# Moving the last three waits of a DMA-bound kernel from SP to GpSimd

## The chip, the cores and the metric

The kernel runs on one core of one Trainium2 chip. The metric is the device time of one execution in microseconds, as it is reported for each run. All runs quoted were fast, with a granted clock of 1.0. The *span* that the profile shows is a different quantity: it runs from the first to the last instruction of the program.

## The reference

```python
B, S, D = 1024, 16, 512          # bfloat16
def reference(x, y, gamma):      # x, y: (B, S, D); gamma: (D,)
    return x + gamma * y
```

Two arrays of 16.8 MB are read and one is written, with one multiplication and one addition for each element.

## The kernel before

The program is written by hand, with one instruction stream for each engine. SP issues the loads, ACT issues the load of gamma and the two stores, VectorE (DVE) multiplies and adds, TensorE (PE) only broadcasts gamma and passes two signals on. GpSimd (POOL) has, apart from its part in the opening barriers and one instruction called INC_SWDGE_SEM, nothing but four small fills that the framework puts at the opening of the program. A helper waits for a semaphore and takes its count off again:

```python
def _take(sem, n, eng):
    return eng.wait_ge(sem, n).then_inc(sem, -n)        # line 25 of the profile
...
SP = [('y', 0, 64), ('x', 0, 64, 0), ('y', 64, 128), ('x', 64, 117, 0), ('x', 117, 128, 64)]
ACT = [('g',), ('s', 0, 64), ('s', 64, 128)]
...
    ring(nc.sync, SP, EARLY[0])      # issues the loads; the first goes ahead of the opening barriers
    ring(nc.scalar, ACT, EARLY[1])   # issues gamma and, when its rows are added, each store
    nc.vector.memset(ones_row, 1.0).then_inc(s_ones, 1)
...
    nc.scalar.sem_inc(s_end, 1)                      # ACT has issued everything
    _take(s_end, 1, nc.sync)
    _take(s_add, n, nc.sync)                         # all additions are done
    _take(s_out, 16 * len(stores), nc.sync)          # both stores have landed: the end of the program
```

The last line holds back the end of the program until all 32 increments of the two stores are in: the last of them came 118.571 us after the span's start, and SP's wait ended at 118.604.

Of the kernel before, what the change touches and what calls it, by code (L numbers as in the profile page):

```python
# [21 lines left out]
def _take(sem, n, eng):  # L22


    return eng.wait_ge(sem, n).then_inc(sem, -n)  # L25


def kernel(
# [9 lines left out]
    nc = tc.nc  # L38
# [9 lines left out]
    n = len(PIECES)  # L48
# [13 lines left out]
    stores = [w for w in SP + ACT if w[0] == "s"]  # L62
# [9 lines left out]
    s_add, s_go, s_rel, s_end, s_out = sem("s_add"), sem("s_go"), sem("s_rel"), sem("s_end"), sem("s_out")  # L72
# [93 lines left out]


    nc.scalar.sem_inc(s_end, 1)
    _take(s_end, 1, nc.sync)
    _take(s_add, n, nc.sync)  # L170
    _take(s_out, 16 * len(stores), nc.sync)

    main = nc.main_func.blocks[0].instructions
    names = {i.name for i in early}
# [35 lines left out]
```

## Time and profile before

| | kernel before |
|---|---|
| reported time, median of 3 | 119.94 us (119.87 to 119.99) |
| span | 118.6 us |
| last of 32 store increments, from the span's start | 118.571 us |
| DMA traffic | 50.33 MB at 424 GB/s over the span; DMA share 0.99, 1.01 and 1.01 in the three stretches of 30 us up to 90 us |
| VectorE busy | 59% |

The lines that the prediction rests on stand in it. The page's groups of DMA issues (what it writes and reads, queue, count, and at the end the median time from issue to landing in us) have this line for the two stores, the second of which is the last transfer:

```profile
out_dram<-y_sb ACTq DMA_DIRECT2D x2, 22.8
```

The opening, in the timeline (start, duration, engine, line, operation):

```profile
0.00 0.37 SPq L116 DMA_DIRECT2D y_sb<-in_y_dram  x1
0.23 0.10 POOL L194 MEMSET const-float32-0.0<- 128x1 f32 x1 [0.23 <-issue]
...
1.52 0.17 DVE L127 MEMSET ones_row<- 1x128 bf16 x1 [1.52 <-PEq L41]
```

The span starts with SP's first load issue. The first instruction that touches data on an engine is GpSimd's fill at 0.23 us, the next VectorE's fill at 1.52.

### The profile page before, as it was taken

What the parts mean: (1) busy time and instruction counts of PE and PEld (TensorE: products, weight loads), DVE (VectorE), ACT (ScalarE), POOL (GpSimd) and SP (SyncE); (2) the same over time, 40 slices, a digit from 0 to 9 for tenths busy, and PEclk for the clock granted to TensorE, in tenths of its full rate; (3) what the DMA queues carried; (4) which work ended last, traced back from release to release, by engine and by line L of the source; (5) the groups of instructions that cost most, each with busy time, mean ns of one, the idle gap of its engine ahead of it and who ended that gap; (6) DMA issues with size and microseconds to landing.
All of it is one profiled execution on the core that took longest, in us unless ns stands there. A gap on an engine that the chain in (4) does not pass through costs nothing. (4 is left out here: it accounts for less than half of the span.)

```text
span 118.6 us, 78 instructions
## 1 busy us (share of the span) xinstructions
PE 0.6 (0%) x1; PEld 0.1 (0%) x1; DVE 70.0 (59%) x10; POOL 0.2 (0%) x4
## 2 busy tenths in 40 slices
PE   0001000000000000000000000000000000000000
PEld 0000000000000000000000000000000000000000
DVE  0002000599999299999759999999999910000000
POOL 0000000000000000000000000000000000000000
DMA  9889888998899888998896969598899888988892
GB/s 354 354 376 685 354 354 354 597 464 354 354 398 663 354 354 354 663 398 354 354 586 293 586 293 567 220 639 354 354 575 486 354 354 376 685 354 354 354 619 88
DMA packets 1010, 50.33 MB, mean 424 GB/s; under 512 B 113, under 2 KB 114, under 8 KB 114
## 3 DMA queue, kind: packets, MB, share of 16 engines
q1 hardware_dynamic: 720, 33.55, 66.0%
q10 hardware_dynamic: 290, 16.78, 32.6%
HBM read 33.56 MB, written 16.78 MB: 424 GB/s over the span
## 5 line engine op out<-in xcount | busy, mean ns | idle before, releaser
L156 DVE TENSOR_TENSOR y_sb<-y_sb,gamma_sb 128x27136 bf16<-128x27136 bf16 (+1 forms) x4 | 34.6, 8688 | 12.7 <-DVEq L25 12.7
L165 DVE TENSOR_TENSOR y_sb<-x_sb,y_sb 128x27136 bf16<-128x27136 bf16 (+1 forms) x4 | 34.6, 8688 | 2.3 <-DVEq L25 2.2
L132 DVE CAST gamma_sb<-gamma_ps 128x512 bf16<-128x512 f32 x1 | 0.7, 692 | 8.8 <-DVEq L25 8.8
L127 DVE MEMSET ones_row<- 1x128 bf16 x1 | 0.2, 165 | 1.5 <-PEq L41 1.5
L130 PE MATMUL gamma_ps<-gamma_row,ones_row 1*128 1x512 bf16 x1 | 0.6, 578 | 9.7 <-PEq L25 9.7
L130 PEld LDWEIGHTS gamma_ps<-gamma_row,ones_row 1*128 1x128 bf16 x1 | 0.1, 100 | 9.7 <-issue 9.7
L194 POOL MEMSET const-uint8-127<- 128x1 uint8 x1 | 0.1, 102 | 0.0
L194 POOL MEMSET const-bfloat16-1.0<- 128x1 bf16 x1 | 0.1, 101 | 0.0
L194 POOL MEMSET const-float32-0.0<- 128x1 f32 x1 | 0.1, 98 | 0.2 <-issue 0.2
L194 POOL MEMSET const-float32-1.0<- 128x1 f32 x1 | 0.1, 98 | 0.0
## 6 DMA issues: line engine op xcount, KB each, us to landing
x_sb<-in_x_dram SPq DMA_DIRECT2D x1, 6784.0 KB, 20.8
x_sb<-in_x_dram SPq DMA_DIRECT2D x1, 1408.0 KB, 23.9
y_sb<-in_y_dram SPq DMA_DIRECT2D x2, 40.2
out_dram<-y_sb ACTq DMA_DIRECT2D x2, 22.8
x_sb<-in_x_dram SPq DMA_DIRECT2D x1, 39.7
gamma_row<-in_gamma_dram ACTq DMA_DIRECT2D x1, 1.0 KB
```

The lines of the kernel that those rows point to most:

```text
L127: nc.vector.memset(ones_row, 1.0).then_inc(s_ones, 1)
L130: nc.tensor.matmul(gamma_ps, ones_row, gamma_row, start=True, stop=True).then_inc(s_ps, 1)
L132: nc.vector.tensor_copy(out=gamma_sb, in_=gamma_ps).then_inc(s_dve, 1)
L156: nc.vector.tensor_tensor(out=yt, in0=yt, in1=g, op=MULT).then_inc(s_dve, 1)
L165: nc.vector.tensor_tensor(out=yt, in0=xt, in1=yt, op=ADD).then_inc(s_add, 1)
L194: nc = _bacc.Bacc("TRN2", target_bir_lowering=False, num_devices=1)
```

## The change

GpSimd is idle for the whole body (0.2 us busy, in the four fills, the last of which ends at 0.43 us), so it is to do the waiting. SP then ends with its last load, issued at 56.1 us.

```diff
     nc.scalar.sem_inc(s_end, 1)
-    _take(s_end, 1, nc.sync)
-    _take(s_add, n, nc.sync)
-    _take(s_out, 16 * len(stores), nc.sync)
+    _take(s_end, 1, nc.gpsimd)
+    _take(s_add, n, nc.gpsimd)
+    _take(s_out, 16 * len(stores), nc.gpsimd)
```

## The prediction

The marks, here and in two of the expectations, show where passages are cut. The records show clearing in blocks of consecutive numbers, of which that of 7 to 53 ends last (119.117 to 119.465 us), but not which engine clears which.

> **What bounds the kernel now.** I read the page from the top, then the same end of the span cut into stretches, then SP's own waits, then the line that holds every wait, and last the semaphore records that lie behind these views. First the header and the slices:
>
> ```profile
> span 118.6 us, 78 instructions
> ...
> DVE  0002000599999299999759999999999910000000
> POOL 0000000000000000000000000000000000000000
> DMA  9889888998899888998896969598899888988892
> GB/s 354 354 376 685 354 354 354 597 464 354 354 398 663 354 354 354 663 398 354 354 586 293 586 293 567 220 639 354 354 575 486 354 354 376 685 354 354 354 619 88
> DMA packets 1010, 50.33 MB, mean 424 GB/s; under 512 B 113, under 2 KB 114, under 8 KB 114
> ```
>
> The DMA row is full from the first slice to the last but one, while VectorE is idle in the last seven slices and GpSimd all along. So 50.33 MB of traffic sets the time, and what comes after it is a tail. The stretches at the end (columns: length, busy time of PE, PEld, DVE and POOL, clock, DMA share, GB/s):
>
> ```profile
> 95.00:98.00 3.00, 0.00 (x0) 0.00 (x0) 0.36 (x1) 0.00 (x0) 1.00 0.81 350
> 98.00:118.00 20.00, 0.00 (x0) 0.00 (x0) 0.00 (x0) 0.00 (x0) 1.00 0.97 419
> 117.00:118.60 1.60, 0.00 (x0) 0.00 (x0) 0.00 (x0) 0.00 (x0) 1.00 0.01 0
> ```
>
> From 98 us on nothing runs but the second store. It was issued by ACT at 95.40 us and takes some 23 us. Who waits for it is in the DMA queue's own waits and in the line of the waits:
>
> ```profile
> SPq L25 <- SPq L25: 62.0, 2, 39.3
> ...
> L25 DVEq EVENT_SEMAPHORE  x9: 21/21/21, 10.4 to 80.0; - x9
> L25 PEldq EVENT_SEMAPHORE  x3: 51/51/51, 1.7 to 76.6; - x3
> L25 SPq EVENT_SEMAPHORE  x3: 17/17/17, 95.8 to 118.6; - x3
> L25 ACTq EVENT_SEMAPHORE  x1: 17/17/17, 76.8 to 76.8; - x1
> ```
>
> SP's three waits are those at issue: the first two pass at 95.8 us, right behind ACT's last issue, and the third, for the stores, at 118.6 us, which is where the span ends. (The releaser named in the wait view is a program line, not the store; the landing records below show the store.) The chain of waits adds nothing here: its last entry is the last addition.
>
> The rest I take from the trace's semaphore records, in us from the span's start. The last of the 32 store increments lands at 118.571; SP's wait runs from 118.587 to 118.604. The span stops there, but the reported time, 119.93 for the profiled execution, is 1.33 longer. What follows in the records: five updates of semaphore 2 at 118.736, 118.779, 118.817, 118.852 and 118.899; then all other semaphores cleared, from 118.849 to 119.465; then nine more updates of semaphore 2, from 119.689 to 120.046. So the tail behind the last store is about 1.4 us, and the reported time evidently contains most of it. The change can act only on this tail.
>
> [...]the nine updates at the end span 357 ns, and the clearing falls into five interleaved blocks of about 51 numbers.[...]GpSimd's waits in the opening barriers took 17 ns[...].[...] the records show 2 x 16 increments, so either engine has to wait for the same last one.
>
> **The change part by part.** The order of shown instructions is the same on all engines; only three waits move from SP to GpSimd.
>
> 1. First two waits: they pass at about 95.8 us, 22.8 us before the last landing. Cost 0 on either engine.
>
> 2. SP ends early. Its last load is issued at 56.1 us, and then it has only the closing barrier to wait in. ACT shows that this is safe: it issues the last store at 95.40 and, by the records, steps into the barrier at 96.01, while the store runs on for 22.6 us. I expect 0 for the transfers.
>
> 3. The third wait on GpSimd. In the opening barriers, before the body, an engine's wait starts some time after the increment that releases it: 25 ns on GpSimd (update at one record, wait at the next), 17 on SP. Start to start of two waits in a row is 78 ns on GpSimd and 70 on SP. From landing to SP's step into the barrier it is 118.736 - 118.571 = 165 ns. GpSimd's analogue: 165 + 8 + 8 = 181. Added: 0.016 us.
>
> 4. The order of the barrier, where I expect the cost. The first update of semaphore 2 in the body comes 0.235 us after PE's last instruction, the second 0.224 after ACT's, the next two follow 39 and 43 ns later, and the fifth, alone, comes after SP's wait. So the order up is PE, ACT, GpSimd, DVE, SP, and down again DVE, GpSimd, ACT, PE (which engine is third and which fourth[...] is an inference). SP is the turning point. When it comes last, only the way down is left: 118.736 to 118.899, 163 ns. With GpSimd last, its own step up, DVE's step up, SP's turn and the whole way down are left. The records have such a case, in the barrier 2.7 us before the span's start, where the third update came late: its seven remaining updates follow at 43, 24, 112, 39, 34 and 50 ns, in sum 302 ns. The long 112 is DVE's: it had just stepped up and needs 136 ns from there to its next step, though SP's turn is in the middle. Added: 302 - 163 = 0.139 us.
>
> 5. PE is the last to leave the first barrier,[...] and is the first that the final barrier needs (119.689). So a later release of PE moves everything behind it one for one.
>
> Sum: 0.016 + 0.139 = 0.155 us on 119.94, that is **120.10 us**, 0.13% longer.
>
> **The rivals.** (a) *Nothing arrives.* If the reported time ends with the last wait, or the waiting hides the step up, only the 0.016 us of term 3 remain: 119.95. For it: the origin of the 1.33 us is my reading. Against: a figure that stops at the wait would be near 118.6. (b) *SP has work of its own after its program*, which it now does early, hidden. The 132 ns from the end of its wait to its barrier step is the most it could be; a gain of at most 0.1, 119.84. Against: PE and ACT show even longer gaps (235 and 224 ns), so this is probably common to all engines and GpSimd would have it too. (c) *GpSimd ends heavily*: one of its drains in the opening took 181 ns against 8 on ACT. If such a thing stands on its way out, it adds another 0.15 to 0.2: 120.3. Its later drains, with no memsets before them, took 41 and 34 ns, which speaks against. (d) *The transfers shift* because SP has gone: a new order on the queues could move the last landing by a few tenths either way, 119.6 to 120.3. Step 2 speaks against, and the issue order does not change.
>
> **Range and chances.** The three timings of before lie from 119.87 to 119.99, so 0.06 either way is plain scatter, less for a median. Term 4 is measured on one event and rests on an inferred order; it could be 0 or, with (c), double. I take 119.90 to 120.35. A change of over 2% would be 2.4 us, longer than the whole 1.4 us tail, so a gain of that size is impossible from the tail, and a loss would need something that no record shows. Faster 0.004, same 0.986, slower 0.010.
>
> **What would show it right or wrong.** Right: the last store increment at the same 118.57 within a tenth or two; GpSimd's third wait within 30 ns of it; semaphore 2 then stepping up three times more and down four times, with a gap over 100 ns in the middle, some 0.30 us in all instead of 0.163; the clearing and final barrier unchanged in shape and later by that much; and the span itself, which ends at the wait, almost unchanged (118.6). Term 3 is wrong if GpSimd takes over 60 ns longer than SP from landing to barrier. Term 4 is wrong if four updates follow GpSimd's as they followed SP's. Step 2 is wrong if the landings of loads or stores moved by more than the scatter. The prediction fails if the time is below 119.90, which would point to (b) or (d), or above 120.35, which would point to (c).

## The result, and the profile after

The changed kernel took 120.66 us (median of 6 runs, 120.57 to 120.77) against 119.97 us (119.87 to 120.01) of the kernel before in the same rounds. The ratio is 1.0058, with a 95% interval from 1.0045 to 1.0071. A ratio here is the mean time of one kernel's fast runs over that of the other's of the same rounds, so it isn't quite the ratio of the medians. The change is within 2%, but clearly slower, by 0.69 us where 0.16 was predicted, and outside the predicted range.

The page of the changed kernel, first the header and the slices:

```profile
span 118.8 us, 78 instructions
...
DVE  0002000699999299999759999999999910000000
POOL 0000000000000000000000000000000000000000
DMA  9899888998899888988896979598899888988891
GB/s 353 353 420 640 353 353 353 662 397 353 353 530 530 353 353 375 684 353 353 353 585 292 548 329 548 238 638 353 353 552 508 353 353 375 684 353 353 353 662 44
```

Slice by slice it's nearly the kernel before. The span grew by 0.2 us only, not by 0.69. The stretches at the end (length, busy time of PE, PEld, DVE and POOL, clock, DMA share, GB/s) are as before too:

```profile
95.00:98.00 3.00, 0.00 (x0) 0.00 (x0) 0.41 (x1) 0.00 (x0) 1.00 0.81 350
98.00:118.00 20.00, 0.00 (x0) 0.00 (x0) 0.00 (x0) 0.00 (x0) 1.00 0.97 419
117.00:118.80 1.80, 0.00 (x0) 0.00 (x0) 0.00 (x0) 0.00 (x0) 1.00 0.01 0
```

The line of the waits shows that the change was made as meant, and that the last wait still ends the span (engine, count, duration in ns, first and last start):

```profile
L25 DVEq EVENT_SEMAPHORE  x9: 21/21/21, 10.2 to 80.1; - x9
L25 PEldq EVENT_SEMAPHORE  x3: 51/51/51, 1.7 to 76.8; - x3
L25 POOLq EVENT_SEMAPHORE  x3: 17/17/17, 95.9 to 118.8; - x3
L25 ACTq EVENT_SEMAPHORE  x1: 17/17/17, 77.0 to 77.0; - x1
```

SP's row is gone, and POOL has it, with the same 17 ns. None of these views shows where 0.5 us went. It lies behind the span, in the semaphore records of the trace. After its last instruction each engine steps into a barrier, seen as updates of semaphore 2. There are nine of them for five engines: the first five are the engines' steps up, and the other four, within 163 ns of SP's step in before, are read as the same order down again. In the changed kernel two come before GpSimd's (77.388 and 96.050 us) and six follow it. With the last landing as the origin, the tail divides as follows, in ns:

| part of the tail | before (SP waits) | after (GpSimd waits) | difference |
|---|---|---|---|
| last landing to the start of the wait | 16 | 23 | +7 |
| the wait instruction | 17 | 17 | 0 |
| end of the wait to the waiter's step into the barrier (its *exit*) | 132 | 562 | +430 |
| from that step to the last step of the barrier | 163 | 285 | +122 |
| clearing of semaphores, up to the final barrier's first step | 790 | 788 | -2 |
| the final barrier | 357 | 357 | 0 |
| sum | 1475 | 2032 | +557 |

So 0.557 of the 0.69 us are in the tail, and 0.43 of them between GpSimd's last instruction and its next sign of life. The other 0.13 us would be in the body: the last store landed 118.756 us after the span's start, 0.185 later than before in these two single profiles.

### The profile page after: what moved, and what is told of

Its sections match the earlier page's. It is cut to its first block, busy times and chain, and to the rows that moved or that the text cites. A ratio compares the mean times of both kernels' runs of the same rounds, so it can differ in the third digit from the quotient of the medians.

```text
span 118.8 us, 78 instructions
## 1 busy us (share of the span) xinstructions
PE 0.6 (0%) x1; PEld 0.1 (0%) x1; DVE 70.0 (59%) x10; POOL 0.2 (0%) x4
```

## The experiments

The theory after the result (A, later G1): GpSimd has a fixed exit of 0.56 us, where SP has 0.13, and the rest of the tail is the barrier's order. Its rivals: all engines but SP are like that (B); GpSimd is slow to go on after a long wait (G2); its exit is long because it ran the opening fills (G3); its exit is work that it could also do while it waits or between simple instructions (G4); it is a cost of being last (G5); it undoes what its opening instruction set up (G6). For the 0.13 us in the body there was scatter (S) against an effect of SP's early end (T). Eleven runs were made, on two chips, all with correct results; each is compared with the kernel before.

### c_before: the kernel before, unchanged

> The kernel before once more, unchanged, for the spans of its executions. In the profile of the change the span (to the end of the last wait) was 118.80 us against 118.60, and the last store landed 118.756 us after the span's start against 118.571. Theory S (scatter[...]): the spans of this run lie between 118.5 and 118.9 and overlap with those of the change (118.7 to 118.9), so that the 0.19 us need no cause. Rival T (the change slows the transfers): all spans here lie at 118.5 to 118.65. Time 119.9 to 120.0, and time less span 1.33 us under both.

It took 120.14 us (119.93 to 120.26, 6 runs), against 120.11 us (119.99 to 120.5, 11 runs) of the same kernel; ratio 0.9997. The six spans lie from 118.6 to 118.9 us, and those of the eleven runs beside it from 118.7 to 119.2. Time less span was 1.28 to 1.37 us throughout, while the spans wandered. So executions of one and the same kernel differ by more than the 0.13 us in question; theory S holds so far. The expected time, 119.9 to 120.0 us, was missed, and the eleven runs beside it go over the band of expected spans at the top. The scatter of 0.06 us that the prediction had taken from three runs was too small too.

### end_act, end_dve, end_pe: the same three waits on the other engines

```diff
-    _take(s_end, 1, nc.sync)              # and the two waits behind it
+    _take(s_end, 1, nc.scalar)            # end_act; nc.vector: end_dve; nc.tensor: end_pe
```

> ACT takes the three last waits. Theory A (GpSimd alone has some 0.43 us of exit between its wait and its step into the barrier; the other engines have SP's 0.13 to at most 0.24): ACT steps 0.13 to 0.24 us after the end of its wait, the barrier then needs 0.32 us instead of SP's 0.163 (the way up from ACT and all the way down), time 120.1 to 120.25. Rival B (SP is the exception, every engine with a datapath pays some 0.56): the step comes 0.5 us or more after the wait, time 120.5 to 120.7.

> VectorE takes the three last waits. Theory A: the step comes 0.13 to 0.24 us after the end of the wait, the barrier then needs 0.24 us (SP's turn and the way down, with DVE's own pause of some 0.1), time 120.0 to 120.2. Rival B: step after 0.5 us or more, time 120.4 to 120.6.

> TensorE takes the three last waits. Theory A: the step comes 0.13 to 0.24 us after the end of the wait, the barrier then needs all its 0.36 us, time 120.15 to 120.35. Rival B: step after 0.5 us or more, time 120.55 to 120.75.

All three ran beside c_before. By the semaphore records, in ns:

| waiter | exit | step to end of the barrier | tail | time, us (median) | ratio to before (95%) |
|---|---|---|---|---|---|
| SP (c_before) | 132 | 163 | 1476 | 120.14 | 0.9997 (0.9984 to 1.0010) |
| DVE (end_dve) | 183 | 241 | 1617 | 120.27 | 1.0008 (0.9994 to 1.0023) |
| ACT (end_act) | 145 | 322 | 1650 | 120.16 | 1.0000 (0.9983 to 1.0017) |
| PE (end_pe) | 235 | 357 | 1816 | 120.34 | 1.0015 (1.0000 to 1.0029) |
| GpSimd (the change) | 562 | 285 | 2032 | 120.66 | 1.0058 (1.0045 to 1.0071) |

The last row is from the first comparison. It was run at another time. Each exit is from one profiled run; those of SP and GpSimd came out the same to 1 ns in every other run where that engine waits last.

Rival B falls: three more engines have exits of 145 to 235 ns, and only GpSimd needs 562. The barrier's part behaves as the order PE, ACT, GpSimd, DVE, SP says: the earlier an engine's place, the more steps are left when it comes last (357, 322, 285, 241 and 163 ns). The order itself, of which two places were an inference, is now shown: in end_dve two steps stand right behind ACT's end (96.18 and 96.22 us) and only the fourth waits for VectorE, and in end_pe none comes before PE's. The times alone would not have decided it; ACT's 0.17 us longer tail doesn't show in its ratio, because the spans happened to be short. The records of the tail repeat to a few ns (1473 to 1476 in the four profiles in which SP waits last), the times to a few tenths of a us (119.99 to 120.5 in the eleven runs beside these).

### c_after: the change once more

> The kernel of the change once more, unchanged. The tail from the last landing to the last update of semaphore 2 should again be 2.03 us against 1.475 of before (0.56 more), and time less span 1.87 against 1.33. Theory S (the transfers are not touched, their 0.19 us in the first profiles was scatter): over the timed executions the spans of this kernel and of before have means within 0.1 us of each other and the ratio of times is 1.0046, 0.56 us. Rival T (SP's early end slows the transfers too): spans longer by 0.1 to 0.2 us, ratio 1.0055 or more.

It took 120.59 us (120.50 to 120.78, 5 runs) against 120.01 us (119.91 to 120.5, 9 runs); ratio 1.0049 (1.0036 to 1.0063). The tail was 2032 ns again, with an exit of 562. The mean span was 118.72 us in its 5 runs and 118.76 in the 9 of the kernel before, and time less span was 1.84 to 1.91 against 1.29 to 1.36. The difference is thus in the tail, 0.56 us, and none of it shows in the transfers. Five spans against nine, with a scatter of tenths, wouldn't decide about 0.1 us alone. But over all timed executions the mean span is 118.73 us in the 35 where SP leaves early and 118.79 in the 41 where it waits to the end (two chips; pool_more, whose increments lengthen the span, is left out). Rival T, which asks for 0.1 to 0.2 us more, falls, and the 0.13 us of the first comparison were scatter.

### pool_more: four instructions behind GpSimd's last wait

```diff
     _take(s_out, 16 * len(stores), nc.gpsimd)
+    s_more = sem("s_more")
+    for _ in range(4):
+        nc.gpsimd.sem_inc(s_more, 1)
```

> The kernel of the change, with four increments of an unused semaphore behind GpSimd's last wait. Theory G1 (a fixed exit behind GpSimd's last instruction): the increments start some 80 ns apart right behind the wait, and the step into the barrier comes 0.5 to 0.57 us after the last of them ends, so the tail is longer than that of the change by 0.3 to 0.4 us and the time some 121.0. Rival G2 (GpSimd is slow to go on after a long wait): the first increment comes 0.4 us or more after the wait, and the step 0.13 to 0.25 us after the last, so that part of the increments replaces nothing and the time is 120.8 to 120.95; the records of the increments tell them apart, not the time. Rival G4 (the exit is work that GpSimd can do while it waits or executes simple instructions): step at most 0.25 us after the last increment and no late first one, time 120.6 to 120.7.

It took 120.92 us; ratio 1.0075 (1.0061 to 1.0089). The line of the new instructions (start in us from the span's start at the end of the line):

```profile
L174 POOLq EVENT_SEMAPHORE  x4: 17/17/17, 118.8 to 119.0; - x4
```

The wait starts at 118.701 us, and the four increments follow at steps of 78, 79, 78 and 78 ns. GpSimd goes on at once after its 22 us of waiting, so rival G2 falls. The last increment ends 0.313 us after the wait, and the step comes 562 ns after that, so the exit is paid behind whatever is last, and the four increments took nothing off it; rival G4 falls with it. The tail grew by 316 ns, from 2032 to 2348. The time itself lies in the band that was expected for G2 (120.8 to 120.95); it is the records that decide.

### pool_clean: no opening fills on GpSimd

```diff
     main = nc.main_func.blocks[0].instructions
+    for i in [i for i in main if "emset" in str(getattr(i, 'opcode', '')) + type(i).__name__]:
+        main.remove(i)
     names = {i.name for i in early}
```

> The kernel of the change without GpSimd's four small opening fills[...]. Theory G1: the step still comes 0.56 us after the wait, time as the change, 0.56 us above before. Rival G3[...]: the step comes 0.13 to 0.25 us after the wait and the time is 0.1 to 0.25 us above before.

The exit was 561 ns and the tail 2035: whether GpSimd ran fills at the opening doesn't matter, and G3 falls. GpSimd's first drain at the opening, behind the fills, did react: 34 ns instead of 181. But the reported time was **119.31 us** (119.15 to 119.44), ratio 0.9941, which no theory had expected. The records say that nothing became faster: the span was 118.80 us, the last landing came 118.759 us after SP's first load issue, and the tail was as long as ever. Time less span fell to 0.55 to 0.64 us. The opening of this kernel:

```profile
0.00 0.37 SPq L116 DMA_DIRECT2D y_sb<-in_y_dram  x1
...
1.51 0.17 DVE L127 MEMSET ones_row<- 1x128 bf16 x1 [1.51 <-PEq L41]
```

With the fills gone, the first data instruction of any engine starts at 1.51 us instead of 0.23, 1.28 later. From SP's first issue to the last update of semaphore 2 it is 120.794 us in this run, and the reported time of the same run is 119.40. That is 1.39 us less, where in the kernels with the fills it is 0.11 to 0.12 less. The difference, again 1.28, suggests that the reported time is counted from the first data instruction.

### one_fill and before_clean: where the count starts

```diff
+    for i in [i for i in main if "emset" in type(i).__name__][1:]:    # one_fill, on the change
+        main.remove(i)
```
```diff
+    for i in [i for i in main if "emset" in type(i).__name__]:        # before_clean, on the kernel before
+        main.remove(i)
```

> The kernel of the change with the first of GpSimd's four opening fills kept and the other three removed. All kernels with the fills so far had a reported time 0.112 to 0.121 us shorter than the stretch from SP's first load issue to the last update of semaphore 2; the one without fills had it 1.39 us shorter, and the next data instruction there, VectorE's fill, starts 1.28 us after the first GpSimd fill. Theory M (the count of the reported time starts at the first data instruction of any engine): one fill is enough, the time is that of the change, 120.5 to 120.7, and time less that stretch is -0.10 to -0.20. Rival N (each fill costs the program some 0.32 us somewhere): time 119.6 to 119.75.

> The kernel before without the four fills. Theory M: reported 1.28 us less than before, 118.65 to 118.85, while nothing in the program comes earlier: last landing 118.5 to 118.95 us after SP's first issue, tail 1.475 us, and the stretch from SP's first issue to the last update of semaphore 2 as in before, 120.0 to 120.3. Rival N: the stretch itself is shorter by over 1 us.

With one fill left, at 0.23 us, the time was 120.64 us (ratio 1.0049), that of the change. The three other fills are worth nothing in it (120.59 us with all four in c_after), and the one that comes first is worth all of the difference to the 119.31 without any:

```profile
0.00 0.37 SPq L116 DMA_DIRECT2D y_sb<-in_y_dram  x1
0.23 0.10 POOL L196 MEMSET const-float32-0.0<- 128x1 f32 x1 [0.23 <-issue]
```

The kernel before without fills reported 118.82 us (118.73 to 119.16; ratio 0.9905). Its last landing was at 118.739 us, its tail 1474 ns, and from SP's first issue to the last update it took 120.213 us, against 120.211 in c_before. Theory M holds and N falls. This version "beats" both kernels in the metric and in nothing else: the last landing and the last update come when they came before, and only the count, it seems, is started later. I don't count it as an improvement.

### pool_hidden: GpSimd's exit beside the stores

```diff
     nc.scalar.sem_inc(s_end, 1)
+    s_hid = sem("s_hid")
+    nc.scalar.sem_inc(s_hid, 1)
+    _take(s_hid, 1, nc.gpsimd)
     _take(s_end, 1, nc.sync)                # and SP's other two, unchanged
```

> The kernel before, with one more wait on GpSimd, for an increment of ACT that comes right behind its last issue, 22 us ahead of the stores' landing; SP still waits for the stores and ends last. Theory G1: GpSimd steps into the barrier 0.5 to 0.6 us after its wait, and not 0.04 us after ACT's step as in the kernel before; that is hidden, and the time is that of before within 0.06 us (time less span 1.33). Rival G5 (the cost is a matter of being last, or of the stores' semaphore, not of GpSimd's exit): GpSimd steps within 0.25 us of its wait.

The waits of this kernel:

```profile
L25 SPq EVENT_SEMAPHORE  x3: 17/17/17, 96.0 to 118.9; - x3
...
L25 POOLq EVENT_SEMAPHORE  x1: 17/17/17, 96.1 to 96.1; - x1
```

ACT steps into the barrier at 96.186 us. GpSimd's step used to follow it within 39 ns; now it comes at 96.643, 561 ns after the end of GpSimd's own wait. So the exit is GpSimd's also where GpSimd isn't last and waits for no store, and G5 falls. It lies under the running store: the tail is 1473 ns, and time less span is 1.29 to 1.37 us as in before. The median, 120.20 us with a ratio of 1.0013 (0.9997 to 1.0029), misses the expected 0.06 us because two of the four spans were 119.0; the interval holds equality.

### pool_bare: nothing of its own on GpSimd

This is pool_clean, with GpSimd's one opening instruction, INC_SWDGE_SEM, removed as well:

```diff
+    for i in [i for i in main if "IncSwdge" in type(i).__name__]:
+        main.remove(i)
```

> The kernel of the change with GpSimd's four fills and its one opening instruction INC_SWDGE_SEM removed, so that the program gives GpSimd nothing but barriers and the three waits. Theory G1 in its plain form (the exit is not the program's doing): GpSimd steps 0.56 us after its wait, tail 2.03 us, reported time 119.2 to 119.5 as without the fills. Rival G6 (the exit undoes or awaits what INC_SWDGE_SEM set up): step after 0.13 to 0.25 us, tail 1.6 to 1.75 us, reported time 118.8 to 119.1.

The exit was 562 ns, the tail 2033, and the time 119.26 us, as in pool_clean. G6 falls. Nothing that was added to or taken from GpSimd's program changed its exit: it was 561 or 562 ns in all seven runs that show it.

## Why the prediction was wrong

**Right: what bounds the kernel, and that only the tail can move.** The transfers were not touched (c_after: mean spans of 118.72 and 118.76 us), and step 2, that SP may leave early, is confirmed by the 35 executions in which SP leaves early (118.73 us against 118.79).

**Right: step 4, the order of the barrier; step 5 fits.** Predicted were 0.139 us for GpSimd's earlier place, from one late third step in the opening; measured were 0.122 (285 against 163 ns). The way to read it was the right one (the "seven remaining updates" of its example are six; its six gaps and their sum are right), and the inferred order was confirmed by end_dve and end_pe. In every kernel 787 to 791 ns lie between the last step of the barrier, PE's, and the first of the final one, as step 5 says. That it is PE's release which sets them isn't shown, since the steps of VectorE, GpSimd and ACT just before it move with it.

**Wrong: step 3, "The third wait on GpSimd".** It put GpSimd's stretch from landing to step at "165 + 8 + 8 = 181" ns. Measured were 602 (23 + 17 + 562). The wake-up, 8 ns, was right within a nanosecond or two. The other 8 ns were the mistake: the spacing of two instructions on GpSimd (78 ns against SP's 70) was taken for the difference of the *exits*. It was also misread: the 78 ns lie between a wait and an increment, where SP's 70 lie between two waits. Two waits in a row on GpSimd, which the changed kernel has, start 95 ns apart (95.856 and 95.951 us). An exit isn't a spacing of instructions. It is the time between the engine's last instruction and its step into the barrier, and each engine has its own here: 132 ns on SP, 145 on ACT, 183 on VectorE, 235 on PE, 562 on GpSimd. GpSimd's couldn't be read from the trace of before, where its program ended at 1.3 us and its step was held back by ACT's until 96.0. The trace did show 235 ns on PE beside SP's 132, hence that exits differ; the prediction used this, and 224 ns on ACT, only to argue that all are alike. The 224 aren't ACT's exit, though: in pool_hidden ACT has one more increment and yet steps 609 ns after the start of its last store issue, as in before, so the step seems to be held there by the issue and not by the last instruction.

**The rivals.** Rival (c), "GpSimd ends heavily", was the one that came true. It was priced at 0.15 to 0.2 us after a drain of 181 ns in the opening, which had nothing to do with it: in pool_clean that drain took 34 ns and the exit was the same. So its direction came true, and its reason did not. The term measures 0.43 us. Rivals (a) and (b) fell with the time itself, which rose by more than the wake-up and didn't fall; (d) fell with c_after.

**The range.** With 0.43 in place of 0.008 in step 3 the sum is 0.007 + 0.430 + 0.122 - 0.002 = 0.557 us, 120.50 on 119.94. The other 0.16 us up to the measured 120.66 are scatter of the body, shown for the kernel before by spans from 118.6 to 119.2 us. The range was too narrow on both counts: an unmeasured exit was given 0.2 us at most, and three runs were taken for the whole scatter.

**What stays open.** The runs show that the 562 ns are GpSimd's, fixed, and behind its last instruction, but not what it does in them: no instruction is recorded there. Nor do they show why the spans of one kernel scatter by some tenths of a us. That the count of the time starts at the first data instruction is read from the one shift of 1.28 us, which three kernels without fills have and all others lack; its end then lies 0.11 to 0.12 us behind the last update of semaphore 2.

## What to carry to other kernels

Let the program end on the engine with the shortest way out, not on the idlest one: here SP, whose exit is 0.13 us and which stands last in the closing barrier, while idle GpSimd cost 0.56 us. (ACT, VectorE and PE, at 0.14 to 0.34 us more than SP, differ from it clearly in the records only.) An engine that sat in a barrier behind another in the profile has shown nothing of its own cost, so a term for it needs a wide band or a run of its own. When time and span disagree, subtract them run by run: it separated a tail that repeats to a few ns from a body that scatters by tenths, and it exposed a gain of 1.2 us in the reported time (118.82 us against 119.99) behind which nothing ended earlier (120.213 us from first issue to last update against 120.211).
